# A scheduled attention-and-experts kernel: row maxima scaled on ScalarE, one memset less, and a new order table

## The chip, the cores and the metric

The kernel runs on one core of a Trainium2 chip. A core has five engines that work at the same time, each strictly in the order of its own instruction list: TensorE (PE, products), VectorE (DVE), ScalarE (ACT), GpSimd (POOL) and SyncE (SP, which issues transfers). They wait for each other by semaphores. The metric is the device time of one execution in microseconds (us); lower is better.

## The reference

What is computed, cut to what matters: windowed attention with four sink keys, whose output rows go through a layer of eight experts with two experts for each row.

```python
# q, k, v: (4 batches, 8 heads, 768, 64); n_sink = 4, window = 128
scores = scale * np.matmul(q, k.transpose(0, 1, 3, 2))      # scale = 1 / 8
is_sink = pos[None, :] < n_sink
rel = pos[:, None] - pos[None, :]
scores = np.where(is_sink | ((rel >= 0) & (rel < window)), scores, -1e9)
a = np.exp(scores - scores.max(-1, keepdims=True))
x = matmul(a / (a.sum(-1, keepdims=True) + 1e-9), v)        # rows x: (3072, 512)
logits = x @ w_gate + np.log1p(np.exp(x @ w_noise)) * noise # 8 experts
top2, top2_w = two largest logits of a row, softmax over the two
for e in range(8):                                          # w1: 512 x 1024, w2: 1024 x 512
    out[rows that chose e] += top2_w * (np.maximum(x @ w1[e], 0) @ w2[e])
```

## The kernel before

**Two parts.** Part one is the attention of all four batches, and, for the first three, the routing (which rows go to which expert) and the first gathers of rows. It ends near 172 us. Part two routes the last batch and runs the experts. Both parts share the one clock: part two's operations follow part one's on each engine without a break.

**Steps of the attention.** Heads are taken in pairs, 4 pairs a batch, 16 pairs in all. A step n is 256 queries of one pair; there are 3 steps to a pair, 48 in all. The chain of a step:
- `qk` (L467): TensorE writes scores to one of two PSUM tiles S.
- `cur` (L472, or L474 to L478): VectorE merges the window's two key blocks by masks. The first step of each pair (16 of the 48) has no block before its first one, so there it adds a mask (L474) and overwrites the four sink columns with a large negative value (L475, a memset).
- `mins` (L481): VectorE takes the row maxima, mn. `lowest` (L484): GpSimd multiplies them by -1/8, giving nb (128 partitions by 4).
- `exps` (L489): ScalarE computes four exponentials with nb as bias, and their sums. From there TensorE transposes the probabilities (L525), ScalarE or VectorE copies them (CT, L531, L528), GpSimd or VectorE masks them (CM, L540, L538).
- The four sink columns take a way of their own: copied on ScalarE (L512), their low part formed on GpSimd, and transposed on TensorE (L520) into a PSUM tile X, of which there are three. `pv` (L550, L553) adds the window's products there; dv, the difference of neighbouring blocks of values, is a GpSimd subtraction of 128x640 (recorded at L374, as all of that helper's calls are).
- The result is copied, transposed back and scaled by VectorE into `strip` (L589); that empties X, and the strip goes to DRAM.

**Routing** of a batch is a chain of some fifty small operations (L840 to L988) on VectorE, GpSimd and ScalarE, 6 rows of 8 experts per partition. Its middle: the masks of the chosen experts, m (L867), are counted by TensorE (L875); VectorE forms the place of each row in its expert's list (L917 to L925: 12 columns, among them an and, L922, and a shift, L923, over integers), compares it with a ramp to build wide selection masks (L929, 128x768; L933, 128x336), which GpSimd multiplies with the row numbers (L936) ahead of the product that makes the lists.

**What sets the order.** Operations are handed to a `Plan` with an engine, an estimated duration, a priority and a kind; kind `PORT` marks an operation of which the plan lets only one run at a time over VectorE and GpSimd. In part one the order on each engine is not found by the plan: a table `ORDER` lists the numbers of the operations of each engine, and `in_order` issues them so. While doing that it keeps a clock of its own from the estimated durations, and where that clock shows TensorE idle near the start it puts in filler products (L1821) that compute nothing that is used:

```python
            if ops[i][6] == PORT:
                port = t + d
            start[i] = t
            if e == "PE":
                if idle and t < idle[0]:
                    w = max(free[e], idle[1])
                    fill += [w] * int((t - w) / (idle[2] * (2 if t < self.cold else 1)))
```

Part two is put in order by the plan itself (a list scheduler), with the same kinds of estimates; it takes over the clock that `in_order` ended with. A gather of rows is issued by GpSimd, and `lat` is the time that the plan sets for its landing.

## Time and profile before

| | us |
|---|---|
| median of 3 runs | 723.29 (723.13 to 725.91) |
| the profiled execution | 725.0, span 723.4 |
| TensorE busy | 694.0 (96% of the span) |
| VectorE busy | 536.4 (74%) |
| ScalarE busy | 398.7 (55%) |
| GpSimd busy | 288.4 (40%) |

The profiled execution is one more run, beside the three. Its span is what the engines' records cover; the rest of its time lies around them. Busy shares are means over both parts, whose limits differ, so the stages have to be read one by one. All times in the rows are microseconds from the span's start unless marked ns.

### The profile page before, as it was taken

How to read it: one execution, taken by the hardware profiler on the slowest of the kernel's cores; microseconds unless marked ns; L12 is line 12 of the kernel's file. 1: busy time of each engine (PE TensorE's matmuls, PEld its weight loads, DVE VectorE, ACT ScalarE, POOL GpSimd, SP SyncE). 2: the span in 40 equal slices, each digit the busy share in tenths (PEclk: the TensorE clock that was granted, in tenths of full speed). 3: DMA queues.
4: the chain of work that ended last, by engine and by line, in shares of the span. 5: the costliest groups of instructions: out<-in, count | busy, mean ns of one | idle time of the engine just before them, and what ended most of it. 6: DMA issues, size and time to landing. Idle time of an engine off the chain costs nothing. (4 is left out here: it accounts for less than half of the span.)

```text
span 723.4 us, 13584 instructions
## 1 busy us (share of the span) xinstructions
PE 694.0 (96%) x4752; PEld 586.1 (81%) x4752; DVE 536.4 (74%) x1292; ACT 398.7 (55%) x1067; POOL 288.4 (40%) x431
## 2 busy tenths in 40 slices
PE   7999898988999999999999999999999999999995
PEld 3767666766778889889988998898899889889984
DVE  6789899877734897797797779587967968785720
ACT  5898787855113465555564566365555645654420
POOL 4547577683336352173224215230722530081022
PEclk9999999999999999999999999999999999999998
DMA  7584878847468997477538564864676291254132
GB/s 250 173 252 162 256 207 219 226 104 257 132 188 230 295 291 214 150 137 231 191 85 221 154 193 109 198 176 140 148 196 198 79 251 55 88 112 106 60 44 45
DMA packets 87335, 123.40 MB, mean 171 GB/s; under 512 B 18656, under 2 KB 55392, under 8 KB 87264
## 3 DMA queue, kind: packets, MB, share of 16 engines
q1 hardware_dynamic: 75856, 94.64, 42.1%
q0 software_dynamic: 11408, 27.86, 19.2%
q8 instruction: 38, 0.62, 0.4%
q14 instruction: 33, 0.27, 0.1%
HBM read 81.75 MB, written 40.73 MB: 169 GB/s over the span
## 5 line engine op out<-in xcount | busy, mean ns | idle before, releaser
L1413 POOL DMA_INDIRECT out<-tmp,idx x34 | 80.5, 2366 | 162.2 <-ACT tmp L1398 153.9
L1520 PE MATMUL B<-x,wr 128*128 128x384 f32 (+1 forms) x392 | 134.8, 344 | 1.5 <-DVE x L374 1.5
L1550 PE MATMUL Y<-w2a,hb 128*128 128x512 f32 x504 | 129.2, 395 | 0.0
L1550 PE MATMUL Y<-w2b,hb 128*128 128x512 f32 x504 | 125.4, 392 | 0.7 <-DVE hb L1543 0.7
L1550 PEld LDWEIGHTS Y<-w2b,hb 128*128 128x128 f32 x504 | 94.4, 188 | 21.1 <-DVE hb L1543 1.2
L1550 PEld LDWEIGHTS Y<-w2a,hb 128*128 128x128 f32 x504 | 94.2, 188 | 19.3
L489 ACT ACTIVATE cbuf<-S,nb 128x132 f32<-128x132 f32 x192 | 68.7, 375 | 23.0 <-POOL nb L484 22.7
L1519 PE MATMUL B<-xe,wr 128*128 128x384 f32 (+1 forms) x224 | 76.9, 343 | 1.0 <-ACT tmp L1534 1.0
L1520 PEld LDWEIGHTS B<-x,wr 128*128 128x128 f32 x392 | 73.6, 188 | 5.0 <-DVE x L374 2.3
L1521 PE MATMUL B<-xe,wr 128*128 128x384 f32 (+1 forms) x224 | 76.7, 343 | 0.0
L374 DVE TENSOR_TENSOR wr<-st,wr 128x512 fp32r<-128x512 f32 (+1 forms) x86 | 59.5, 698 | 14.3 <-ACT wr L1231 14.0
L1519 PE MATMUL B<-x,wr 128*128 128x384 f32 (+1 forms) x168 | 57.9, 345 | 1.0 <-DVE tmp L1537 1.0
L1521 PE MATMUL B<-x,wr 128*128 128x384 f32 (+1 forms) x168 | 57.6, 343 | 0.0
L1231 ACT ACTIVATE wr<-st 128x512 fp32r<-128x512 f32 x84 | 52.0, 624 | 8.8 <-DVE st L374 6.5
L1082 POOL COPY spacer<-hb 1x1 f32<-1x1 f32 x38 | 12.5, 328 | 92.5 <-ACT hb L1540 89.6
L1534 ACT ACTIVATE tmp<-B 128x384 f32<-128x384 f32 (+1 forms) x56 | 28.0, 500 | 38.7 <-PE B L1521 34.7
L1398 ACT ACTIVATE tmp<-Y,wc 128x512 f32<-128x512 f32 x31 | 21.3, 688 | 45.7 <-PE Y L1550 33.4
L467 PE MATMUL S<-kq 64*64 64x196 f32 (+2 forms) x768 | 41.7, 328 | 4.2 <-ACT cbuf L489 4.1
L1519 PEld LDWEIGHTS B<-xe,wr 128*128 128x128 f32 x224 | 42.1, 188 | 3.6 <-ACT tmp L1534 1.3
L1413 POOL DMA_INDIRECT out<-turned,idx x17 | 30.1, 1769 | 37.0 <-ACT turned L1398 33.7
L1521 PEld LDWEIGHTS B<-xe,wr 128*128 128x128 f32 x224 | 42.0, 188 | 0.2
L1067 POOL DMA_INDIRECT sg<-x_rows,rt_idi x30 | 30.5, 1018 | 27.7 <-DMA x_sorted<-sg 12.9
(313 smaller groups left out, 1560.7 us busy)
## 6 DMA issues: line engine op xcount, KB each, us to landing
st<-in_w1c SPq DMA_DIRECT2D x32, 512.0 KB, 4.5
st<-in_w2c SPq DMA_DIRECT2D x32, 512.0 KB, 4.4
kq<-in_qk_t SPq DMA_DIRECT2D x15, 780.0 KB, 5.7
...
x_rows<-strip SPq DMA_DIRECT2D x48, 128.0 KB, 3.5
```

The costliest lines, as they stand in the source:

```text
L374: eng.tensor_tensor(out, a, b, op=OP.subtract)
L467: nc.tensor.matmul(whole[x, h, c0:c1], kq(g)[r, KS + 128 * j + 64 * s:KS + 128 * j + 64 * s + 64], kq(g)[r, o + c0:o + c1], start=True, st ...
L489: nc.scalar.activation(C(n)[:, u], S_(n, 0, KW)[:, u // 2, u % 2], AF.Exp, scale=1.0 / math.sqrt(D), bias=get("nb", n)[:, u // 2, u % 2:u ...
L1067: nc.gpsimd.indirect_dma_start(out=stage(), out_offset=None, in_=xbuf, in_offset=bass.IndirectOffsetOnAxis(ap=cst["idw"]()[:, sh.TE * e + ...
L1231: plan.op("ACT", .03 + .255 * m, z, lambda: nc.scalar.activation(h(), src(), AF.Copy), r=[st], w=[(*key, b)] + old, u=[key, ex], lat=P2["s ...
L1398: nc.scalar.activation(get("y", Y[e, t], [128, DM]), get("Y", Y[e, t]), AF.Copy, scale=c["wc"][e % 2][:, t:t + 1])
L1413: d = nc.gpsimd.indirect_dma_start(out=out, out_offset=bass.IndirectOffsetOnAxis(ap=c["idx"][:size(e, t), e, t:t + 1], axis=0), in_=get("y ...
L1519: nc.tensor.matmul(p, wh, h, start=start and not k, stop=False, skip_group_check=True)
L1520: nc.tensor.matmul(p, wh, l, start=False, stop=False, skip_group_check=True)
L1521: nc.tensor.matmul(p, wl, h, start=False, stop=k == 1, skip_group_check=True)
L1534: nc.scalar.activation(u_of(e, k), src(), AF.Copy)
L1550: nc.tensor.matmul(p, h[:, x * (CAP + R) + 128 * t:x * (CAP + R) + 128 * t + 128], w[:, y], start=(f == 0 and x + y == 0), stop=(f == FC - ...
```

## The change

The scaled row maxima are computed by ScalarE instead of GpSimd. The mask added in the first steps becomes 132 columns wide, its last four filled with the large negative value, so that the addition covers the sink columns too and the memset goes; the set-up gains a memset of the wider mask and one for each of the two tiles S, whose sink columns the addition now reads. In the plan, many small operations of the routing (L840 to L1015), the row sums and the copy of the gate weights become `PORT`; estimated durations change a little; landings of the first gathers are set at 5.4 and 4 us for 4.2 and 3. The table `ORDER` of part one is replaced.

```diff
 ORDER = dict(
-    Pool=(0, 17, 13, 26, 55, 22, 34, 28, 68, 32, 95, 70, 64, 76, 103, 59, 74, 105, 111, 135, 99, 143, 109, 170, 183,
+    Pool=(13, 34, 22, 32, 28, 76, 59, 74, 64, 105, 111, 99, 70, 145, 151, 109, 139, 131, 185, 149, 191, 225, 179, 189,
...
-    m0 = consts.tile([128, 128], F32, name="m0")
-    nc.vector.tensor_scalar(m0, jp, 0.0, -BIG, op0=OP.is_gt, op1=OP.mult)
+    m0 = consts.tile([128, KW], F32, name="m0")
+    nc.vector.memset(m0, -BIG)
+    nc.vector.tensor_scalar(m0[:, :128], jp, 0.0, -BIG, op0=OP.is_gt, op1=OP.mult)
...
-            nc.vector.tensor_tensor(S_(n, 0, 128)[:, 0], S_(n, KW, 128)[:, 0], m0[:, None, :].to_broadcast([128, 2, 128]), op=OP.add)
-            nc.vector.memset(S_(n, 128, NS)[:, 0], -BIG)
+            nc.vector.tensor_tensor(S_(n, 0, KW)[:, 0], S_(n, KW, KW)[:, 0], m0[:, None, :].to_broadcast([128, 2, KW]), op=OP.add)
...
     def lowest(n):
-        nc.gpsimd.tensor_scalar(get("nb", n, [128, 2, 2]), get("mn", n), -1.0 / math.sqrt(D), None, op0=OP.mult)
+        nc.scalar.activation(get("nb", n, [128, 2, 2]), get("mn", n), AF.Copy, scale=-1.0 / math.sqrt(D))
...
-            op("DVE", .6 if jj else .8, n + P(n, "cur"), lambda n=n: cur(n), w=[("S", n)])
+            op("DVE", .61 if jj else .98, n + P(n, "cur"), lambda n=n: cur(n), w=[("S", n)])
             op("DVE", .62, n + .4 + P(n, "mins"), lambda n=n: mins(n), r=[("S", n)], w=[("mn", n)])
-            op("Pool", .15, n + .4 + P(n, "sub"), lambda n=n: lowest(n), r=[("mn", n)], w=[("nb", n)])
+            op("ACT", .17, n + .4 + P(n, "sub"), lambda n=n: lowest(n), r=[("mn", n)], w=[("nb", n)])
...
-            op("ACT", 1.55, n + .4 + P(n, "exps"), lambda n=n: exps(n), r=[("S", n), ("nb", n)], w=[("C", n), ("sm", n // 2)])
+            op("ACT", 1.4, n + .4 + P(n, "exps"), lambda n=n: exps(n), r=[("S", n), ("nb", n)], w=[("C", n), ("sm", n // 2)])
...
-                op("Pool", .15, n + .8 + P(n, "sums"), lambda m=m: sums(m), w=[("sm", m)])
+                op("Pool", .25, n + .8 + P(n, "sums"), lambda m=m: sums(m), w=[("sm", m)], kind=PORT)
...
-    dve(lambda: v.tensor_scalar(rt("pp", pair, I32), rt("g"), 127, None, op0=OP.bitwise_and), ["g"], ["pp"], .08)
+    dve(lambda: v.tensor_scalar(rt("pp", pair, I32), rt("g"), 127, None, op0=OP.bitwise_and), ["g"], ["pp"], .09, kind=PORT)
...
-        plan.op("Pool", 1.28, z, go, r=[("idg", int(not first))] + kept * first, w=[row], lat=4.2 if first else 3)
+        plan.op("Pool", 1.28, z, go, r=[("idg", int(not first))] + kept * first, w=[row], lat=5.4 if first else 4)
...
-    plan.op("DVE", .065, z, go, r=[row], w=[("wc", e, t)], u=[("wc", e)])
+    plan.op("DVE", .08, z, go, r=[row], w=[("wc", e, t)], u=[("wc", e)], kind=PORT)
...
                     nc.vector.memset(s[:64, :, a * sh.HALF + sh.NS + 192:a * sh.HALF + sh.NS + 256], 0.0)
+                nc.vector.memset(s[64:, :, sh.HALF + 2 * sh.NS:sh.HALF + 3 * sh.NS], 0.0)
```

What the new table and the moved operation do to the instruction lists is shown at three places, one in the routing of each of the first three batches. After the change, lines from 395 to 473 have numbers higher by one (cur's L472 is L473, its addition L475); from L476 on they are as before. In the names, sm are the row sums, ri their reciprocals, pcbuf the sink columns, z and rt_w the weights of the experts.

GpSimd in the routing of the first batch, up to the dv that stands there, before the change:

```order
L484 TENSOR_SCALAR nb<-mn 128x4
L493 TENSOR_SCALAR sm<-sm 128x8
L374 TENSOR_TENSOR pcbuf<-cbuf,pcbuf 128x16x4
L885 TENSOR_TENSOR z_121<-rt_mx 128x6
L484 TENSOR_SCALAR nb<-mn 128x4
L374 TENSOR_TENSOR dv<-vn 128x640
```

The same stretch after it:

```order
L867 TENSOR_TENSOR m<-oh_122 128x48
L540 AFFINE_SELECT CM<-CT 128x512
L885 TENSOR_TENSOR z_123<-rt_mx 128x6
L540 AFFINE_SELECT CM<-CT 128x512
L493 TENSOR_SCALAR sm<-sm 128x8
L374 TENSOR_TENSOR dv<-vn 128x640
```

The two multiplications nb (L484), each of which waited for row maxima of VectorE, are gone; the one that stood last ahead of dv has only a mask and row sums in its place.

VectorE in the routing of the second batch, before the change (rt_g is a row's place, rt_pp and rt_tq its and and shift, rt_tv a value made of the shift):

```order
L923 TENSOR_SCALAR rt_tq<-rt_g 128x12
L925 SCALAR_TENSOR_TENSOR rt_tv<-rt_tq,rt_vl 128x12
L504 RECIPROCAL ri<-sm 128x4x2
L933 TENSOR_TENSOR rt_tc_1961<-io_94,rt_tv 128x336
L933 TENSOR_TENSOR rt_tc_1964<-io_94,rt_tv 128x336
L474 TENSOR_TENSOR S_83<-S_83,m_167 128x2x128
L475 MEMSET S_83 128x2x4
L476 COPY_PREDICATED S_83<-le,S_83 128x2x128
L478 TENSOR_TENSOR S_83<-S_83,m_169 128x2x4
L922 TENSOR_SCALAR rt_pp<-rt_g 128x12
L481 TENSOR_REDUCE mn<-S_83 128x4
L589 TENSOR_TENSOR strip<-B_78,ri 128x256
```

The same stretch after the change:

```order
L923 TENSOR_SCALAR rt_tq<-rt_g 128x12
L922 TENSOR_SCALAR rt_pp<-rt_g 128x12
L925 SCALAR_TENSOR_TENSOR rt_tv<-rt_tq,rt_vl 128x12
L929 TENSOR_TENSOR rt_op_1955<-io,rt_pp 128x768
L933 TENSOR_TENSOR rt_tc_1967<-io_96,rt_tv 128x336
L504 RECIPROCAL ri<-sm 128x4x2
L475 TENSOR_TENSOR S_83<-S_83,m_169 128x2x132
L476 COPY_PREDICATED S_83<-le,S_83 128x2x128
L478 TENSOR_TENSOR S_83<-S_83,m_172 128x2x4
L589 TENSOR_TENSOR strip<-B_78,ri 128x256
L481 TENSOR_REDUCE mn<-S_83 128x4
L589 TENSOR_TENSOR strip<-B_79,ri 128x256
```

L922 stood nine rows behind L923, right ahead of a row maximum (L481) and two strips (the second is the row behind the last one shown); it now stands right behind L923, with an L929 and one L933 after it, and the two strips no longer follow each other. On GpSimd, the same batch from the copy of a block of expert weights (wr) on, before:

```order
L374 TENSOR_TENSOR wr<-st,wr 128x1024
L484 TENSOR_SCALAR nb<-mn 128x4
L889 TENSOR_TENSOR z_121<-z_121 128x6
L867 TENSOR_TENSOR m<-oh_123 128x48
L540 AFFINE_SELECT CM<-CT 128x512
L885 TENSOR_TENSOR z_124<-rt_mx 128x6
L890 TENSOR_TENSOR rt_wd<-oh_120,z_121 128x96
L892 TENSOR_TENSOR rt_w<-rt_wd 128x48
L493 TENSOR_SCALAR sm<-sm 128x8
L484 TENSOR_SCALAR nb<-mn 128x4
L374 TENSOR_TENSOR pcbuf<-cbuf,pcbuf 128x16x4
```

The rows that follow there:

```order
L887 TENSOR_SCALAR rt_den<-z_124 128x6
L540 AFFINE_SELECT CM<-CT 128x512
L936 TENSOR_TENSOR rt_tc_1961<-rt_tc_1961,tok 128x336
L540 AFFINE_SELECT CM<-CT 128x256
L374 TENSOR_TENSOR dv<-vn 128x640
L493 TENSOR_SCALAR sm<-sm 128x8
```

After the change, from the masks m on:

```order
L867 TENSOR_TENSOR m<-oh_125 128x48
L540 AFFINE_SELECT CM<-CT 128x512
L374 TENSOR_TENSOR wr<-st,wr 128x1024
L374 TENSOR_TENSOR pcbuf<-cbuf,pcbuf 128x16x4
L540 AFFINE_SELECT CM<-CT 128x512
L892 TENSOR_TENSOR rt_w<-rt_wd 128x48
L493 TENSOR_SCALAR sm<-sm 128x8
L936 TENSOR_TENSOR rt_tc_1967<-rt_tc_1967,tok 128x336
L540 AFFINE_SELECT CM<-CT 128x256
L885 TENSOR_TENSOR z_126<-rt_mx 128x6
L374 TENSOR_TENSOR dv<-vn 128x640
L540 AFFINE_SELECT CM<-CT 128x512
```

The wr stood ahead of m and stands behind it now. There is one L936 ahead of dv in both; in the new lists the L936 waits for the L933 that stands behind L922 on VectorE, while in the old ones both L933 stood ahead of L922.

VectorE in the routing of the third batch, before:

```order
L924 TENSOR_SCALAR rt_vl<-r_128 128x12
L922 TENSOR_SCALAR rt_pp<-rt_g 128x12
L923 TENSOR_SCALAR rt_tq<-rt_g 128x12
L925 SCALAR_TENSOR_TENSOR rt_tv<-rt_tq,rt_vl 128x12
L929 TENSOR_TENSOR rt_op_2632<-io,rt_pp 128x768
L933 TENSOR_TENSOR rt_tc_2639<-io_94,rt_tv 128x336
L933 TENSOR_TENSOR rt_tc_2644<-io_94,rt_tv 128x336
L907 TENSOR_TENSOR vm<-slot,B_79 128x4
L589 TENSOR_TENSOR strip<-B_77,ri 128x256
```

After the change:

```order
L924 TENSOR_SCALAR rt_vl<-r_130 128x12
L923 TENSOR_SCALAR rt_tq<-rt_g 128x12
L922 TENSOR_SCALAR rt_pp<-rt_g 128x12
L925 SCALAR_TENSOR_TENSOR rt_tv<-rt_tq,rt_vl 128x12
L929 TENSOR_TENSOR rt_op_2622<-io,rt_pp 128x768
L933 TENSOR_TENSOR rt_tc_2626<-io_96,rt_tv 128x336
L929 TENSOR_TENSOR rt_op_2635<-io,rt_pp 128x768
L933 TENSOR_TENSOR rt_tc_2653<-io_96,rt_tv 128x336
L589 TENSOR_TENSOR strip<-B_77,ri 128x256
```

Ahead of the strip stood one L929 and two L933; now two of each stand there. On ScalarE, each set of four exponentials (L489) now has its nb (L484) ahead of it on the same engine.

## Rows read from the trace of the kernel before

**Rows 1.** the page: busy time, share of the span and instructions of each engine.
```profile
PE 694.0 (96%) x4752; PEld 586.1 (81%) x4752; DVE 536.4 (74%) x1292; ACT 398.7 (55%) x1067; POOL 288.4 (40%) x431
```

**Rows 2.** table by stage (from:to us): length, busy (instructions) per engine, clock, DMA.
```profile
0.00:16.40 16.40, 11.74 (x107) 5.50 (x108) 10.51 (x36) 8.28 (x32) 7.16 (x27) 1.00 0.79 276
16.40:56.00 39.60, 38.80 (x547) 27.66 (x548) 33.06 (x75) 34.82 (x158) 19.14 (x43) 1.00 0.62 197
56.00:96.00 40.00, 36.40 (x521) 27.16 (x521) 37.57 (x102) 30.98 (x143) 25.78 (x52) 1.00 0.64 201
96.00:136.00 40.00, 37.73 (x543) 27.58 (x543) 36.99 (x103) 32.18 (x139) 28.33 (x57) 1.00 0.87 245
136.00:172.00 36.00, 31.84 (x396) 23.94 (x395) 27.25 (x84) 21.75 (x77) 25.43 (x53) 1.00 0.62 177
```

**Rows 3.** what TensorE waits for, whole span: total us, times, longest us.
```profile
PE B L520 <- DVE strip L589: 4.4, 5, 1.3
...
PE B L1145 <- DMA xg<-x_rows,idg: 1.7, 1, 1.7
```

**Rows 4.** timeline: start, duration us, engine, line, [idle before <- releaser].
```profile
74.16 0.26 PE L520 MATMUL B<-idr,pcbuf 128*128 128x128 f32 x1 [1.29 <-DVE strip L589]
...
103.89 2.37 POOL L374 TENSOR_TENSOR wr<-st,wr 128x1024 fp32r<-128x1024 f32 x1
...
112.06 1.54 POOL L374 TENSOR_TENSOR dv<-vn 128x640 f32<-128x640 f32 x1
...
112.18 1.44 DVE L922 TENSOR_SCALAR rt_pp<-rt_g 128x12 int32<-128x12 int32 x1
...
114.62 0.28 PE L520 MATMUL B<-idr,pcbuf 128*128 128x128 f32 x1 [1.33 <-DVE strip L589]
...
151.86 0.28 PE L520 MATMUL B<-idr,pcbuf 128*128 128x128 f32 x1 [1.03 <-DVE strip L589]
```

**Rows 5.** two VectorE lines, all runs: shortest/middle/longest ns, first and last start.
```profile
L922 DVE TENSOR_SCALAR rt_pp<-rt_g x3: 173/1444/1486, 69.7 to 147.7; 128x12 int32<-128x12 int32 x3
...
L923 DVE TENSOR_SCALAR rt_tq<-rt_g x3: 159/172/1509, 72.1 to 149.1; 128x12 int32<-128x12 int32 x3
```

**Rows 6.** groups of instructions, 0 to 171 us: busy us, mean ns | idle before.
```profile
L484 POOL TENSOR_SCALAR nb<-mn 128x4 f32<-128x4 f32 x48 | 17.0, 355 | 44.5 <-DVE mn L481 38.3 <-ACT cbuf L489 1.5 <-DVE strip L589 1.3
...
L475 DVE MEMSET S<- 128x8 f32 x16 | 1.0, 65 | 1.2
...
L886 ACT ACTIVATE z<-z 128x6 f32<-128x6 f32 x3 | 0.6, 213 | 0.9 <-POOL z L885 0.9
```

**Rows 7.** timeline of ScalarE, two dependent small instructions.
```profile
175.47 0.24 ACT L842 ACTIVATE turned<-turned 128x48 f32<-128x48 f32 x1 [2.60 <-DVE turned L840]
175.75 0.24 ACT L843 ACTIVATE turned<-turned 128x48 f32<-128x48 f32 x1
```

**Rows 8.** the table by stage for tile nb alone: ScalarE and GpSimd.
```profile
16.40:56.00 39.60, 22.54 (x120) 4.03 (x14) 1.00 0.62 197
```

**Rows 9.** timeline of the start, several engines.
```profile
6.17 0.43 DVE L474 TENSOR_TENSOR S<-S,m 128x256 f32<-128x256 f32 x1 [1.27 <-PE S L467]
...
7.47 1.47 PE L1821 MATMUL B<-one 128*128 128x512 bf16 x6
...
10.11 0.89 PE L467 MATMUL S<-kq 64*64 64x196 f32 x16 [1.18 <-ACT cbuf L489]
...
12.67 1.19 POOL L484 TENSOR_SCALAR nb<-mn 128x4 f32<-128x4 f32 x1 [2.47 <-DVE mn L481]
...
14.56 0.28 PE L520 MATMUL B<-idr,pcbuf 128*128 128x128 f32 x1 [0.72 <-POOL pcbuf L374]
...
15.47 0.89 PE L467 MATMUL S<-kq 64*64 64x196 f32 x16 [0.63 <-ACT cbuf L489]
```

**Rows 10.** timeline early in the second part, VectorE and GpSimd.
```profile
182.54 2.41 POOL L374 TENSOR_TENSOR w2b<-st,w2b 128x1024 fp32r<-128x1024 f32 x1
182.60 2.38 DVE L920 SCALAR_TENSOR_TENSOR turned<-turned,r 128x12 int32<-128x12 uint32 x1
```

More of the change, by code (lines that the diff above doesn't have):

```diff
@@ L840, in routing @@
     dve(lambda: v.scalar_tensor_tensor(rt("ab", ab_), lg()[:, :, E:], -1.0, lg()[:, :, E:], op0=OP.mult, op1=OP.max),
-        lgk, ["ab"])
+        lgk, ["ab"], kind=PORT)
     act(lambda: nc.scalar.activation(rt("ex", ab_), rt("ab"), AF.Exp, scale=-1.0), ["ab"], ["ex"])
@@ L860, in routing @@
     dve(tops, ["no"], ["mx"], .08 * nt)
-    dve(topi, ["no", "mx"], ["ix"], .14 * nt)
+    dve(topi, ["no", "mx"], ["ix"], .14 * nt, kind=PORT)
     full = [128, 2, nt, E]
@@ L952, in routing @@
         n_ = sh.FA
-        gp_ = lambda fn, r, w: step("Pool", .13, fn, [(x, i) for x in r], [(x, i) for x in w])
+        gp_ = lambda fn, r, w: step("Pool", .17, fn, [(x, i) for x in r], [(x, i) for x in w], kind=PORT)
         gp_(lambda: gp.tensor_scalar(tab("em"), tab("vm"), -1.0, 1.0, op0=OP.mult, op1=OP.add), ["vm"], ["em"])
-        step("Pool", .13, lambda: gp.tensor_tensor(tab("ids"), tab("ids"), tab("vm"), op=OP.mult), [("vm", i)], [("ids", 0)])
+        step("Pool", .17, lambda: gp.tensor_tensor(tab("ids"), tab("ids"), tab("vm"), op=OP.mult), [("vm", i)], [("ids", 0)], kind=PORT)
         gp_(lambda: gp.tensor_tensor(tab("ga"), tab("em"), c["dum"].to_broadcast([128, n_]), op=OP.mult), ["em"], ["ga"])
-        step("Pool", .13, lambda: gp.tensor_tensor(tab("ga"), tab("ga"), tab("ids"), op=OP.add), [("ids", 0)], [("ga", i)])
+        step("Pool", .17, lambda: gp.tensor_tensor(tab("ga"), tab("ga"), tab("ids"), op=OP.add), [("ids", 0)], [("ga", i)], kind=PORT)
         gp_(lambda: gp.tensor_tensor(tab("sa"), tab("em"), tab("spare"), op=OP.mult), ["em"], ["sa"])
-        step("Pool", .13, lambda: gp.tensor_tensor(tab("sa"), tab("sa"), tab("ids"), op=OP.add), [("ids", 0)], [("sa", i)])
-        step("Pool", .1, lambda: gp.tensor_copy(c["m"][:, sh.T:, 0], tab("em")), [("em", i)], [("mx", 0)])
+        step("Pool", .17, lambda: gp.tensor_tensor(tab("sa"), tab("sa"), tab("ids"), op=OP.add), [("ids", 0)], [("sa", i)], kind=PORT)
+        step("Pool", .14, lambda: gp.tensor_copy(c["m"][:, sh.T:, 0], tab("em")), [("em", i)], [("mx", 0)], kind=PORT)
         dve(lambda: v.scalar_tensor_tensor(c["idg"][:, fl], where()[:, fl], 128.0, tab("ga"), op0=OP.add, op1=OP.add),
@@ L1007, in ordered @@
     dve(lambda: v.tensor_reduce(rt("ef", [128, E]), rt("pe"), op=OP.add, axis=AX.X), ["pe"], ["ef"], .13, after=9)
-    dve(lambda: v.tensor_copy(c["eid"], rt("ef")), ["ef"], [("eid", 0)], .07, after=9)
+    dve(lambda: v.tensor_copy(c["eid"], rt("ef")), ["ef"], [("eid", 0)], .07, after=9, kind=PORT)
     dve(lambda: v.tensor_tensor(c["vm"], c["slot"], rt("cp")[:, :, None].to_broadcast([128, E, TE]), op=OP.is_lt),
@@ L1014, in ordered @@
     n = E * TE - sh.FA
-    step("Pool", .28, lambda: gp.tensor_scalar(tab("em"), tab("vm"), -1.0, 1.0, op0=OP.mult, op1=OP.add), [("vm", 1)], [("em", 1)])
+    step("Pool", .28, lambda: gp.tensor_scalar(tab("em"), tab("vm"), -1.0, 1.0, op0=OP.mult, op1=OP.add), [("vm", 1)], [("em", 1)], kind=PORT)
     step("Pool", .28, lambda: gp.tensor_tensor(tab("ga"), tab("em"), c["dum"].to_broadcast([128, n]), op=OP.mult), [("em", 1)], [("ga", 1)], kind=PORT)
     step("Pool", .28, lambda: gp.tensor_tensor(tab("sa"), tab("em"), tab("spare"), op=OP.mult), [("em", 1)], [("sa", 1)], kind=PORT)
-    step("Pool", .28, lambda: gp.tensor_scalar(c["over"], c["most"][:1, :1], 0.0, None, op0=OP.is_gt), [("most", 0)], [("over", 0)])
+    step("Pool", .28, lambda: gp.tensor_scalar(c["over"], c["most"][:1, :1], 0.0, None, op0=OP.is_gt), [("most", 0)], [("over", 0)], kind=PORT)
 def experts_setup(nc, cst, sh, pool):
```

24 lines of the change are left out of this document (12 added, 12 removed), and 96 rows, old and new, of tables (ACT, DVE, PE, Pool).

## The prediction, made before the changed kernel was run

> **What bounds the kernel now.** I read the page's engine shares first [rows 1]: TensorE is busy 694.0 us of 723.4, VectorE 536.4. So at most 29.4 us of the span is TensorE waiting, and a change that leaves the products alone can only take from those. The table by stage [rows 2] says where they lie in the first part, up to 172 us: 4.66 us before 16.4 (16.40 less 11.74), then 0.80, 3.60, 2.27 and 4.16, together 15.5. The granted clock is 1.00 in all of them, so the clock plays no role. The same table shows two other engines close to full: VectorE has 37.57 of 40.00 us from 56 to 96 and 36.99 from 96 to 136, ScalarE 34.82 of 39.60 from 16.4 to 56. In the two middle stages VectorE and TensorE are both near their limit, and whatever stretches a VectorE instruction there is paid by TensorE. The list of what TensorE waits for [rows 3] has one named culprit: L520, the sink transpose, waits 4.4 us in five goes for the strip of VectorE (L589), which must empty the PSUM bank first.
>
> The timeline shows why [rows 4]. At 112.06 GpSimd starts the difference of values, dv (1.54 us). At 112.18 VectorE starts L922, an and over 12 columns, and takes 1.44 us for it, ending (113.62) when dv does (113.60). The same line took 0.173 us in its quickest run and L923, a shift of the same size, 0.159; their slowest are 1.486 and 1.509 [rows 5]. So these small instructions are held for the whole length of a GpSimd instruction that meets them. Behind them stand the row maximum and the strip, and TensorE waits 1.33 us until 114.62. It happens in each of the three routed batches: 1.29 us before 74.16, 1.33 before 114.62, 1.03 before 151.86, together 3.65.
>
> **What the change does, part by part.**
>
> *The scaled maxima (L484) go from GpSimd to ScalarE.* GpSimd loses 48 instructions and 17.0 us; they took 355 ns on the mean [rows 6]. ScalarE gains 48 of 4 columns. No such instruction runs there now; the nearest is L886, 6 columns, 213 ns [rows 6]. The exponentials follow it on the same engine and need its result: L842 and L843, two dependent small ones, stand 0.28 us apart (175.47, 175.75) [rows 7]. So a new one takes 0.21 to 0.28 us of ScalarE, 10.2 to 13.4 us in all. In the fullest stage, where 14 of them stand [rows 8], ScalarE goes from 34.82 to 37.8 or 38.7 of 39.60. It still fits; an engine at 96% that works strictly in order will make TensorE wait now and then, and I put 0.5 us on the path there (bounds 0, since it fits, and 3.9, the 14 at 0.28 with no cover). What is hidden is hidden by TensorE's own work of 38.80 us in that stage.
>
> The Trainium skill's page "ScalarE: Activation LUTs" (Rules for kernel authors) speaks against this edit: a multiplication belongs on VectorE, and an ACTIVATE with a bias taken by pointer is to be budgeted at about 0.3 us plus 0.83 ns for each element. By that figure, an estimate from the page, the fullest stage would hold 34.82 + 14 x 0.3 = 39.0 of 39.60. No row of this kernel shows such a multiplication on ScalarE.
>
> The gain lies where GpSimd was held. At 12.67 [rows 9] its nb took 1.19 us beside a VectorE instruction, and TensorE then waited 0.72 us at 14.56 and 0.63 at 15.47. With 0.21 to 0.28 on ScalarE that nb is some 0.9 us shorter. Bounds: 0, and 1.35, both waits; I take 0.8, since the delay taken away is nearer to the upper one. In other places nb's usual way (GpSimd) and the new one cost about the same.
>
> *One memset less in `cur`.* L475 was 16 instructions, 1.0 us busy, with 1.2 us of idle time in front of them [rows 6]. The addition before it now covers 264 columns for 256: by its 0.43 us [rows 9], 0.013 us more, 0.2 in all. VectorE gains 0.8 to 2.0 us over four batches; TensorE sees of that only what falls in the full stages. Bounds 0 and 2.0, I take 0.4, near the lower end, since the waits of those stages come from elsewhere. Three memsets more in the set-up cost nothing: VectorE sat idle 1.27 us before its first addition at 6.17. Without that cover they would cost some 0.3.
>
> *Three more filler products at the start.* The plan's fillers run at 0.245 us each (six in 1.47 us from 7.47), 0.74 us for three. They hide in the 1.18 us in which TensorE waits before 10.11; uncovered they would cost 0.74. I take nothing.
>
> *Port kinds and new durations.* In part one each engine's order is the table's, so these costs do not set it; they count the fillers and hand their clock to part two, which is scheduled with them. What counts in part one is the table.
>
> *The new table at the three collisions.* In batch 0 the old row had nb, which waited for the maxima, directly ahead of dv on GpSimd, so dv came as late as those maxima did, beside the wide L929 and then L923. Now nothing there waits for them; dv can be over when L922 and L923 come. I take 0.9 of the 1.29. In batch 1 the old row had dv free to run beside L922. In the new one dv stands behind L936, which multiplies what L933 makes, and L933 stands behind L922 and L923 on VectorE: those two cannot meet. But a copy of weights (wr), which ran 2.37 us from 103.89 [rows 4], before the mask product m (L867) of this batch, now stands behind m and one L540, and the chain from m to L922 goes on meanwhile; if it is quick, L919 to L922 meet wr. I take 0.8 of the 1.33. In batch 2 dv stands later too, but VectorE now has four wide instructions (two L929, two L933) ahead of the strip where three were, so the strip may be as late as before: 0.2 of the 1.03. Together 1.9; bounds 0 and 3.65.
>
> *The rest of the table.* The first gathers stand a little ahead of where they were against the last mask (L540); the wait for their landing is 1.7 us [rows 3]. Bounds 0 and 1.7; I take 0.2, because four gathers still go out one after the other. The sum of the last pair, which moves behind the gathers, is needed only by the last strips and by the gate sums. All other TensorE waits from 16.4 to 172 come to 10.83 - 3.65 - 1.73 = 5.45 us; a new order drops some and makes others. I take nothing, bounds 2.5 either way, about half.
>
> *Part two.* Its order moves as well. At 182.60 VectorE's L920 took 2.38 us, held by the weight split on GpSimd (2.41 us from 182.54) [rows 10], and now that split starts sooner against the routing. Such shifts move waits of 1 us or so; I take nothing, bounds 1.5 either way. The products there are the same, and TensorE is full, so what part one gains or loses comes out at the end.
>
> **Sum.** -0.8 - 0.4 - 1.9 - 0.2 + 0.5 = -2.8 us. The profiled run took 725.0 us (span 723.4), which would be 722.2; it lies 1.7 above the median of the three, 723.29, and the same step from there gives 720.5.
>
> **Rivals.**
> - *The collisions move instead of going.* dv has to run somewhere, VectorE is 94% full in the stage with two of the three, and four wide instructions now stand together in batch 2. For it: held instructions are seen in every batch, and wr is longer than dv. Against it: the pairs of batches 0 and 1 are parted in the rows. Then -0.8 - 0.4 - 0.2 + 0.5 leaves -0.9: 722.4.
> - *ScalarE becomes the bound, and it gets slower.* nb waits for VectorE's maxima at the head of ScalarE's queue, and the copies behind it wait too. The place is 16.4 to 56: spare there is 4.78 us for 14, so from 0.34 us each it costs. At 0.6 us each it takes 3.6 and eats the gains. At 0.75 it takes 5.7 there and, with 14 taken in the next two stages too, 1.5 from 56 to 96 (30.98 + 10.5 against 40) and 2.7 from 96 to 136 (32.18 + 10.5), 9.9 in all, less the 3.3 gained elsewhere: 729.9. For it: ScalarE's fill and the strict order. Against: 0.21 to 0.28 in the nearest rows, and the exponentials waited for nb at the same place before. The page's budget for an ACTIVATE above would bring the stage to its edge, not over it.
> - *All of it goes.* The three collisions (3.65), both waits at the start (1.35), 0.4 of the memsets and half of the other waits (2.7), less nothing for ScalarE: -8.1, 715.2. For it: these waits have the same few causes. Against: half of those others have no link to the port.
> - *The costs in the plan do nothing.* True for part one by themselves, as said; then only the table and the two edits count, which the forecast has already.
>
> **How the numbers follow.** Forecast, -1.5 to -6: 0.50. Collisions move: 0.25. All goes: 0.13. ScalarE binds: 0.12. The likeliest gives 720.5, with its own range 717.3 to 721.8. The range for 8 in 10 goes from 715.4, near the case in which all goes, to 725.0, past the moved collisions by the 2.5 that the rest of the table may cost; it leaves out most of the ScalarE case and the far end of the other. A change of 0.5% is 3.6 us, about what a measurement here tells from none: faster is below 719.7, slower above 726.9. Of the forecast's -1.5 to -6 half lies below 719.7 (0.25), with 0.13 of the case in which all goes: faster 0.38. Slower 0.11, nearly all of the ScalarE case. The rest, 0.51, is same.
>
> **What would show it.** In the new profile: L484 on ScalarE near 0.21 us, ScalarE at 37 to 39 us in the stage up to 56 with TensorE's waits there below 1.5; L922 and L923 near 0.17 us in batches 0 and 1; L520's waits for the strip down from 4.4 to about 2; TensorE's part one ending 2 to 3 us sooner, and part two as long as before. I am wrong if L919 to L923 still last as long as dv or wr, if TensorE's waits for the exponentials grow by several us, or if part two's waits change by more than 2 us.

## The result, and the profile after

The changed kernel takes 716.61 us (median of 4 runs, 715.63 to 718.88), the kernel before 724.01 (4 runs beside it): ratio 0.9899, 95% interval 0.9867 to 0.9931, 7.4 us faster. Seven further runs on another chip gave 717.72 against 725.02, ratio 0.9907 (0.9874 to 0.9939). The profiled run took 718.88 us, span 717.2.

The page's engine shares, as in [rows 1]:

```profile
PE 692.4 (97%) x4755; PEld 586.5 (82%) x4755; DVE 530.8 (74%) x1279; ACT 403.6 (56%) x1115; POOL 281.4 (39%) x383
```
The table by stage, as in [rows 2]:

```profile
0.00:16.40 16.40, 13.30 (x130) 6.97 (x132) 12.14 (x40) 9.86 (x43) 6.04 (x23) 1.00 0.80 276
16.40:56.00 39.60, 39.21 (x572) 28.95 (x570) 33.91 (x74) 36.81 (x181) 17.53 (x31) 1.00 0.71 220
56.00:96.00 40.00, 39.28 (x565) 29.36 (x558) 38.21 (x104) 35.77 (x163) 21.26 (x43) 1.00 0.72 227
96.00:136.00 40.00, 37.71 (x540) 27.91 (x540) 35.70 (x105) 32.28 (x146) 24.97 (x49) 1.00 0.69 188
136.00:172.00 36.00, 32.76 (x353) 24.60 (x350) 27.65 (x101) 21.67 (x74) 19.53 (x40) 1.00 0.76 228
```
TensorE's waiting in the five stages (length less busy) is 3.10, 0.39, 0.72, 2.29 and 3.24, together 9.7 for 15.5 before. VectorE is as full as it was in the second and third (33.91, 38.21), and ScalarE is fuller: 36.81 of 39.60 and 35.77 of 40.00. Up to 56 us TensorE has done 702 products, before 654; three of the 48 more are fillers. So its lead is larger than its shorter waits; whether short gaps between products, counted as busy, make the difference isn't shown.

What TensorE waits for, as in [rows 3]:

```profile
PE B L1519 <- ACT tmp L1534: 3.5, 3, 2.0
PE B L761 <- DVE strip L589: 1.5, 2, 0.8
PE B L875 <- DVE m L867: 1.4, 1, 1.4
...
PE B L1145 <- DMA xg<-x_rows,idg: 1.2, 2, 0.7
PE S L468 <- ACT cbuf L489: 1.0, 3, 0.4
PE S L468 <- DVE mn L481: 1.0, 1, 1.0
```
L520 no longer waits for the strip. Two waits for a strip stand at the gate product instead (L761, 0.72 us before 126.57 and 0.83 before 159.96), so 4.4 us of such waits have become 1.5. The first and the third row lie in the second part; there the first was 1.0 us in one go before, and the third is new.

The small instructions of [rows 5], with the L920 beside them:

```profile
L920 DVE SCALAR_TENSOR_TENSOR rt_g<-rt_ix,r x3: 174/176/1082, 65.8 to 140.6; 128x12 int32<-128x12 uint32 x3
...
L922 DVE TENSOR_SCALAR rt_pp<-rt_g x3: 156/164/165, 67.5 to 140.9; 128x12 int32<-128x12 int32 x3
...
L923 DVE TENSOR_SCALAR rt_tq<-rt_g x3: 159/172/173, 67.6 to 140.8; 128x12 int32<-128x12 int32 x3
```
L922 and L923 are at 0.16 to 0.17 us in all three batches. The hold is not gone everywhere: one L920, at 65.8, took 1.08 us beside a dv. TensorE waited for no strip there.

The groups of [rows 6] up to 171 us; columns as there:

```profile
L489 ACT ACTIVATE cbuf<-S,nb 128x132 f32<-128x132 f32 x192 | 68.4, 372 | 0.9
...
L484 ACT ACTIVATE nb<-mn 128x4 f32<-128x4 f32 x48 | 10.0, 208 | 11.3 <-DVE mn L481 10.7
...
L475 DVE TENSOR_TENSOR S<-S,m 128x264 f32<-128x264 f32 x16 | 6.9, 434 | 1.6 <-PE S L468 0.8 <-ACT CT L531 0.6 <-ACT pcbuf L512 0.3
```
The new instruction on ScalarE takes 208 ns, 10.0 us in all. Two rows that I had not read in the kernel before are that of the exponentials, same view, and that of all its nb, in the columns of [rows 5]:

```profile
L489 ACT ACTIVATE cbuf<-S,nb 128x132 f32<-128x132 f32 x192 | 68.7, 375 | 23.0 <-POOL nb L484 22.7
```
```profile
L484 POOL TENSOR_SCALAR nb<-mn x48: 212/226/1188, 8.3 to 155.8; 128x4 f32<-128x4 f32 x48
```
Before, ScalarE stood idle for 23.0 us in front of the exponentials (6.3 of them before the first), nearly all for nb from GpSimd. Now it is 0.9 there and 11.3 in front of the nb themselves (5.3 of them before the first), where it waits for the maxima: 12.2 for 23.0. Of these 10.8 us less the nb's own work fills 10.0, so the idle time shows the place and not the size of the gain. The second row shows more of it. Most nb took 0.23 us on GpSimd, and the mean of 355 ns comes from eight that took 0.47 to 1.19, each beside a wide VectorE instruction: the one of 12.67 to 13.86 ran beside VectorE's L426 (12.51 to 13.78).

The last transpose of part one (L580) marks where TensorE leaves the attention. Both kernels, before first (shortest/middle/longest ns, first and last start in us):

```profile
L580 PE MATMUL B<-idf,turned x96: 272/273/329, 21.1 to 166.6; 128*128 128x128 f32 x96
```
```profile
L580 PE MATMUL B<-idf,turned x96: 272/273/330, 18.3 to 158.5; 128*128 128x128 f32 x96
```
Part one ends 8.1 us sooner (166.6 and 158.5), the whole 6.2 in these two executions (spans 723.4 and 717.2). From that transpose to the end it takes 558.7 us where it took 556.8: in these two the second part gives 1.9 us back. One execution says little here. In all traces of the runs below together with these two, the five with the old lists of the second part take 551.4 to 556.8 us from that transpose on (middle 555.1), the seven with the new ones 553.5 to 560.8 (middle 559.6).

### The profile page after: what moved, and what is told of

It is laid out like the page before. It is cut to its first block, busy times and chain, and to the rows that moved or that the text cites. A ratio compares the mean times of both kernels' runs of the same rounds, so it can differ in the third digit from the quotient of the medians.

```text
span 717.2 us, 13573 instructions
## 1 busy us (share of the span) xinstructions
PE 692.4 (97%) x4755; PEld 586.5 (82%) x4755; DVE 530.8 (74%) x1279; ACT 403.6 (56%) x1115; POOL 281.4 (39%) x383
## 4 chain that ended last, share of the span: by engine, by line
PE 74%; DMA 9%; DVE 5%; ACT 3%; issue 3%; POOL 3%; SPq 0%; POOLq 0%; DVEq 0%; ACTq 0%
PE Y L1550 31%; PE B L1519 9%; PE B L1520 9%; PE B L1521 9%; PE S L468 3%; DMA xg<-x_sorted 3%; ACT cbuf L489 2%; DMA x_rows<-strip 2%; PE B L550 2%; DMA sg<-x_rows,idg 2%; PE Y L1553 2%; PE B L525 1%; DMA vn<-in_v 1%; PE B L553 1%; DMA xg<-x_rows,idg 1%
## 5 line engine op out<-in xcount | busy, mean ns | idle before, releaser
L1413 POOL DMA_INDIRECT out<-tmp,idx x34 | 87.1, 2562 | 153.3 <-ACT tmp L1398 149.1
L1519 PE MATMUL B<-xe,wr 128*128 128x384 f32 (+1 forms) x224 | 77.2, 345 | 3.5 <-ACT tmp L1534 2.2
L489 ACT ACTIVATE cbuf<-S,nb 128x132 f32<-128x132 f32 x192 | 68.4, 372 | 0.9
L1519 PE MATMUL B<-x,wr 128*128 128x384 f32 (+1 forms) x168 | 57.9, 345 | 1.3 <-ACT tmp L1534 1.3
L1519 PEld LDWEIGHTS B<-xe,wr 128*128 128x128 f32 x224 | 42.0, 188 | 7.3 <-ACT tmp L1534 3.1
L1413 POOL DMA_INDIRECT out<-turned,idx x17 | 31.9, 1876 | 36.9 <-ACT turned L1398 33.8
L1534 ACT ACTIVATE tmp<-B 128x384 f32<-128x384 f32 (+1 forms) x56 | 27.7, 499 | 32.3 <-PE B L1521 27.8
L1540 ACT ACTIVATE hb<-B 128x384 fp32r<-128x384 f32 (+1 forms) x56 | 28.0, 502 | 27.9 <-DVE B L1537 13.3
```

The costliest lines, as they stand in the source:

```text
L489: nc.scalar.activation(C(n)[:, u], S_(n, 0, KW)[:, u // 2, u % 2], AF.Exp, scale=1.0 / math.sqrt(D), bias=get("nb", n)[:, u // 2, u % 2:u ...
L1413: d = nc.gpsimd.indirect_dma_start(out=out, out_offset=bass.IndirectOffsetOnAxis(ap=c["idx"][:size(e, t), e, t:t + 1], axis=0), in_=get("y ...
L1519: nc.tensor.matmul(p, wh, h, start=start and not k, stop=False, skip_group_check=True)
L1534: nc.scalar.activation(u_of(e, k), src(), AF.Copy)
L1540: nc.scalar.activation(hx(e, f, 0, j), src(), AF.Relu)
```

## The experiments

Each ran beside the kernel before on one chip. "Mean clock" is the mean granted TensorE clock of an execution. The kernel before ran 66 times here: 724.4, 725.0 and 724.7 us on the three chips.

**The maxima on ScalarE, in the old table.** 48 numbers of the table move from GpSimd's row to ScalarE's.

```diff
-        nc.gpsimd.tensor_scalar(get("nb", n, [128, 2, 2]), get("mn", n), -1.0 / math.sqrt(D), None, op0=OP.mult)
+        nc.scalar.activation(get("nb", n, [128, 2, 2]), get("mn", n), AF.Copy, scale=-1.0 / math.sqrt(D))
...
-    Pool=(0, 17, 13, 26, 55, 22, 34, 28, 68, 32, 95, 70, 64, 76,
+    Pool=(0, 13, 22, 34, 28, 32, 70, 64, 76,
...
-    ACT=(19, 12, 27, 21, 33, 56,
+    ACT=(17, 19, 12, 26, 27, 21, 33, 55, 56,
```

> The kernel before, with the scaled maxima on ScalarE, each right ahead of its exponentials; the rest of the old table and all else as before (two more filler products). Theory A (the maxima's shorter way to the exponentials is what pays): 3 to 5 us faster than before, 719 to 721, with the lead already there by the sixteenth step. Theory B (the new table pays, by parting held VectorE instructions from dv): 0 to 1 us faster, 723 to 724. Theory C (ScalarE becomes the bound by itself, and only the new table makes room for it): 1 to 3 us slower.

Measured: 720.47 us, ratio 0.9947 (0.9927 to 0.9967), 3.9 us faster. The exponentials' group up to 171 us, the last transpose, and the first stage:

```profile
L489 ACT ACTIVATE cbuf<-S,nb 128x132 f32<-128x132 f32 x192 | 68.5, 369 | 1.9
```
```profile
L580 PE MATMUL B<-idf,turned x96: 272/273/330, 20.9 to 163.8; 128*128 128x128 f32 x96
```
```profile
0.00:16.40 16.40, 13.21 (x110) 6.74 (x110) 10.70 (x37) 9.07 (x36) 6.11 (x23) 0.90 0.75 276
```
ScalarE's 23 us of waiting fall to 1.9 there (10.7 in front of the nb come to it), and part one ends 2.8 us sooner although TensorE's clock was at 0.90 on the mean in the first stage, which costs up to 0.10 x 16.4 = 1.6 us. Theory A holds for this edit, and C falls. The collisions have no part in it: in batch 0 the hold moved to L920 (1.42 us), and TensorE still waits 1.27, 1.24 and 0.98 us at the three places. The lead was not all there by the sixteenth step, though: that maximum started 1.2 us sooner than before, the last but two 3.5 us sooner, so it grows over part one. Summed over the 48 steps, the way from the end of a maximum to its first exponential is 29.6 us for 34.2. Of these 4.6 us, 4.2 lie at the eight steps whose nb GpSimd took 0.47 to 1.19 us for, 0.3 at the other forty: what pays is mostly that nb is no longer held. No run tests that by itself.

**All but the new table.** The changed kernel with the old table, nb ahead of its exponentials.

```diff
-    Pool=(13, 34, 22, 32, 28, 76, 59, 74,
+    Pool=(0, 13, 22, 34, 28, 32, 70, 64,
...
```

> The changed kernel with the old table, the maxima put right ahead of their exponentials in ScalarE's list: all of the change but the new order of part one (the second part is ordered by the new costs). Theory A: 718 to 720. Theory B: 721 to 723. Theory C: slower than before.

Measured: 720.76 us, 0.9959 (0.9937 to 0.9981), like the run before it, between the ranges of A and B. Part one ends at 161.5:

```profile
L580 PE MATMUL B<-idf,turned x96: 272/273/330, 20.4 to 161.5; 128*128 128x128 f32 x96
```
So in these traces the table is worth 3.0 us in part one on top of the other edits (158.5), A and B each hold for a part, and since a reordered second part comes with it (555.8 us here, in an order that neither kernel has), the time doesn't show what the wide addition does by itself.

**Two VectorE instructions parted from dv.** In the table of the kernel before:

```diff
-        366, 509, 367, 368, 510, 375, 372, 369, 370,
+        366, 509, 367, 368, 369, 510, 375, 372, 370,
...
-        655, 657, 659, 722, 664, 661, 838, 656, 839,
+        655, 657, 656, 659, 722, 664, 661, 838, 839,
```

> The kernel before, with two VectorE instructions moved in its table: L923 of the first routed batch right behind L922, and L922 of the second batch right behind L923; nothing else. Theory B: both are at 0.17 us instead of 1.5, TensorE's two waits for the strip (1.29 and 1.33 us) shrink, 1.7 to 2.6 us faster than before. The rival (the lock moves to the next VectorE instruction that meets dv): 0 to 0.5 us faster.

Measured: 723.38 us, 0.9982 (0.9964 to 1.0000): 1.3 us by the ratio, with an interval that reaches no change. Both lines, then the timeline of batch 0:

```profile
L922 DVE TENSOR_SCALAR rt_pp<-rt_g x3: 172/180/1490, 72.1 to 149.4; 128x12 int32<-128x12 int32 x3
...
L923 DVE TENSOR_SCALAR rt_tq<-rt_g x3: 160/164/175, 72.2 to 150.8; 128x12 int32<-128x12 int32 x3
```
```profile
73.86 2.21 POOL L374 TENSOR_TENSOR dv<-vn 128x640 f32<-128x640 f32 x1
...
74.60 1.50 DVE L924 TENSOR_SCALAR rt_vl<-r 128x12 f32<-128x12 f32 x1
...
76.58 0.25 PE L520 MATMUL B<-idr,pcbuf 128*128 128x128 f32 x1 [1.29 <-DVE strip L589]
```
The moved instructions are quick (the one left at 1.49 is batch 2's). In batch 1 TensorE's wait for the strip is gone (two of 0.29 and 0.58 for exponentials follow). In batch 0 the hold moved to the next small instruction behind the wide ones: L924, 1.50 us, ends with dv, and TensorE waits the same 1.29. So the rival was right for one place, theory B for the other. The Trainium skill's page "SBUF — State Buffer" (SBUF: two separate sides) calls the port pair that VectorE and GpSimd share an exclusive lock for a whole instruction, where the VectorE instruction has two inputs in SBUF or runs in a two-port mode. The trace agrees on the whole instruction, with L924 ending within 0.03 us of dv; L924 has one input, and no run here shows its mode. This run also showed something else:

```profile
0.00:16.40 16.40, 11.78 (x107) 5.42 (x107) 10.56 (x36) 8.90 (x35) 7.44 (x27) 0.95 0.76 276
16.40:56.00 39.60, 38.84 (x517) 28.27 (x517) 30.85 (x67) 31.82 (x144) 17.00 (x41) 0.93 0.60 194
```
The clock was at 0.95 and 0.93 in the first two stages, at 1.00 in the profile before. This execution lost 0.05 x 16.4 + 0.07 x 39.6 = 3.6 us by that at most.

**The maxima back on GpSimd, in the new table.** Their 48 numbers go back to GpSimd's row, at the places that the plan's clock gives.

```diff
...
-        nc.scalar.activation(get("nb", n, [128, 2, 2]), get("mn", n), AF.Copy, scale=-1.0 / math.sqrt(D))
+        nc.gpsimd.tensor_scalar(get("nb", n, [128, 2, 2]), get("mn", n), -1.0 / math.sqrt(D), None, op0=OP.mult)
```

> The changed kernel with the scaled maxima back on GpSimd, at the places that the plan's clock gives; TensorE's and VectorE's order as in the changed kernel. Theory A: 3 to 5 us slower than the changed kernel, 720 to 722. Theory B: 0 to 1 us slower, 716.5 to 718. Theory C: faster than the changed kernel, 714 to 716.

Measured: 724.01 us, 0.9993 (0.9978 to 1.0009), the kernel before's time and slower than each theory had it. The waiting for nb is back:

```profile
L489 ACT ACTIVATE cbuf<-S,nb 128x132 f32<-128x132 f32 x192 | 68.7, 374 | 22.5 <-POOL nb L484 21.9
```
```profile
L580 PE MATMUL B<-idf,turned x96: 272/273/330, 22.2 to 165.0; 128*128 128x128 f32 x96
```
```profile
0.00:16.40 16.40, 13.00 (x108) 7.11 (x108) 10.78 (x37) 8.08 (x30) 7.01 (x25) 0.93 0.79 276
16.40:56.00 39.60, 38.58 (x532) 28.20 (x524) 30.78 (x64) 33.30 (x154) 17.10 (x42) 0.94 0.64 197
```
The clock fell here too, at 0.93 and 0.94, up to 3.5 us, and once more in the second part (334.8 to 338.2 us, up to 1.7). That mixes with the effect, hence the runs with fillers below. Also, nb starts 0.42 us after its maximum on the mean here, 0.20 in the kernel before: the new order was not made for nb on GpSimd.

**The changed kernel again.** No edit.

> The changed kernel itself once more, on the chip of the runs beside it, for more executions of it. Theory D (part of the gain is the granted clock: with TensorE idle for 3.4 us in all between 9 and 16 us, most executions of the kernel before fall to the lower level once near the start, and the changed kernel, idle for 1.8 us there, doesn't): mean clock of 0.996 or more in nearly all executions, 716 to 718. Without theory D its clocks spread like those of the kernel before (21 of 30 below 0.996).

Measured: 717.72 us, 0.9907. Mean clocks 0.998, 0.995, 0.998, 0.995, 0.998, 0.994, 0.994: not nearly all at 0.996, as theory D had it. Of all 11 executions of the changed kernel 4 are below, of the 66 of the kernel before 48, and those 48 take 725.0 us in the median, the other 18 take 723.2. So the clock seems to be part of the gain, but a small one: an estimate from these groups is (48/66 - 4/11) x 1.8 = 0.7 us. It takes all of the difference between the groups for the clock's doing, which no run shows.

**More fillers in the kernel before.**

```diff
-WARM = 13.0
+WARM = 16.0
```

> The kernel before with filler products put in up to 16 us on the plan's clock in place of 13 (8 more, all between 10 and 16 us); every other list as before. Theory D: the mean clock is 0.996 or more in most executions, 1 to 2 us faster than before, 722 to 723.5. Rival: the clock stays as spread as before, and the fillers cost up to 8 x 0.245 = 2 us, 724 to 726.

Measured: 721.26 us, 0.9957 (0.9939 to 0.9975), 3.1 us by the ratio, mean clock 0.997 (10 of 12 at 0.996 or more). In the trace part one ends as before:

```profile
L580 PE MATMUL B<-idf,turned x96: 272/273/330, 20.8 to 166.4; 128*128 128x128 f32 x96
```
So the fillers keep the clock up and are worth 3.1 us, more than either expectation had. The clock, estimated as above, explains (48/66 - 2/12) x 1.8 = 1.0 of these; where the other 2.1 come from is open. In the two traces the clock is at 1.00 near the start in both, and the whole difference lies behind that transpose, in the same lists: 551.4 us for 556.8, with 4.0 us of TensorE's waits for 8.5.

**Fewer fillers in the changed kernel.**

```diff
-WARM = 13.0
+WARM = 10.0
```

> The changed kernel without the 11 filler products behind its second set of scores (8 are left at the very start). TensorE's order is otherwise the same, and the fillers filled a wait, so without theory D the time stays, 716 to 717.5. Theory D: the clock falls near the start in most executions, mean clock below 0.996, 2 to 4 us slower than the changed kernel, 718.5 to 721.

Measured: 718.71 us, 0.9904 (0.9877 to 0.9931). That is the lower edge of what theory D had, but only 1.0 us above the changed kernel beside it, which the intervals don't tell from none. The clock fell as theory D had it (5 of 6 below 0.996), to 0.79 in the first stage:

```profile
0.00:16.40 16.40, 12.04 (x105) 6.75 (x105) 11.38 (x38) 9.43 (x39) 6.30 (x23) 0.79 0.80 276
```
The low clock lay from 8.2 to 15.0 us. From 8 to 15 TensorE was busy 5.67 of 7.00 us, ScalarE 6.59, and part one ended at 157.2, sooner than the changed kernel's 158.5. So here half the clock had no cost that shows, where ScalarE was the fuller engine. The execution with the lowest mean clock of the six (0.989) was the fastest, 714.74.

**Each nb twice.** The same instruction once more, 48 in all.

```diff
         nc.scalar.activation(get("nb", n, [128, 2, 2]), get("mn", n), AF.Copy, scale=-1.0 / math.sqrt(D))
+        nc.scalar.activation(get("nb", n, [128, 2, 2]), get("mn", n), AF.Copy, scale=-1.0 / math.sqrt(D))
```

> The changed kernel with every scaled maximum computed twice on ScalarE (48 instructions of 0.21 us more, 10 us of ScalarE in part one). Rival of the prediction (ScalarE at the edge): 3 to 9 us slower than the changed kernel, 720 to 726, TensorE's waits for the exponentials between 16 and 96 us growing by several us. With room left on ScalarE: 0 to 2 us slower, 716.5 to 719.

Measured: 718.77 us, 0.9931 (0.9901 to 0.9960), 1.1 us above the changed kernel beside it. Three stages:

```profile
16.40:56.00 39.60, 38.22 (x521) 28.00 (x522) 30.69 (x64) 35.64 (x176) 13.10 (x26) 0.94 0.62 196
56.00:96.00 40.00, 38.95 (x550) 28.98 (x550) 37.98 (x103) 36.91 (x168) 22.63 (x44) 1.00 0.69 212
96.00:136.00 40.00, 38.69 (x554) 28.50 (x552) 36.16 (x103) 35.53 (x171) 23.92 (x45) 1.00 0.77 224
```
With 10 us more work ScalarE is 92% full in the second of them, and TensorE waits only 1.38, 1.05 and 1.31 us. In the first, the rival's place, the clock was at 0.94, so that row tests it less well. Part one ends at 163.3 in this trace, 4.8 us later than in the changed kernel's; a low clock up to 56 us explains at most 0.07 x 16.4 + 0.06 x 39.6 = 3.5 of these. The second part, in the changed kernel's lists, took 553.5 us, the least of the seven. So the doubled work is not free in part one, but it costs far less than the 3 to 9 us of a ScalarE that binds.

**Fillers with the changed kernel, with the moved maxima alone, and with the new table alone.** Three kernels; the last two are those of the runs above with the maxima moved.

```diff
-WARM = 13.0
+WARM = 16.0
```

> The changed kernel with filler products up to 16 us on the plan's clock (8 more), as in the run that did so with the kernel before. If the clock near the start still costs the changed kernel something in some executions (4 of 11 were below 0.996): mean clock 0.997, 0.5 to 1.5 us faster than the changed kernel, 715.5 to 717, faster than both kernels. Rival (its waits there are too short to hold fillers): fillers delay work, 0 to 2 us slower, 717 to 719.

> The kernel before with the scaled maxima on ScalarE and fillers up to 16 us: against the kernel before with the fillers alone (721.3) it shows what the moved maxima do in the old table without a fall of the clock. Chain theory (a shorter way from maximum to exponentials, worth 3 us at the end of part one in the trace): 718 to 719. If most of the 3.8 us were the clock: 720.5 to 721.5.

> The changed kernel with the maxima on GpSimd and fillers up to 16 us. Its first run stood at 724.0 with a low clock in 11 of 12 executions. If the new table is of use without the moved maxima: 718 to 720, below the kernel before with the same fillers (721.3). If the new table needs ScalarE's maxima: 721 to 723.

Measured: 719.64 us (0.9934, 0.9919 to 0.9948), 718.18 (0.9917, 0.9894 to 0.9940) and 725.10 (1.0005, 0.9987 to 1.0024). The last transposes, in this order:

```profile
L580 PE MATMUL B<-idf,turned x96: 272/273/330, 17.9 to 156.6; 128*128 128x128 f32 x96
```
```profile
L580 PE MATMUL B<-idf,turned x96: 272/273/330, 20.8 to 163.3; 128*128 128x128 f32 x96
```
```profile
L580 PE MATMUL B<-idf,turned x96: 272/273/331, 19.4 to 163.1; 128*128 128x128 f32 x96
```
The moved maxima are worth 3.1 us once more, with the clock up: 718.18 against 721.26 (2.9 by the ratios, since the chips differ), and 163.3 against 166.4 at the end of part one. The new table with the wide addition ends part one 3.3 us sooner too (163.1 against 166.4), so it doesn't need ScalarE's maxima there, against the theory; its time is no better all the same, since what follows takes 560 us (723.3 - 163.1), with a fall of the clock from 332.6 to 336.0. The changed kernel with more fillers has the shortest part one of all (156.6) and is slower than without: 716.8 - 156.6 = 560.2 us follow. Both expectations of a gain failed, and in the traces both gains are lost in the second part.

**The old costs in the second part.** Wherever the second part uses them, the costs and kinds are those of before, but for the 5.4 us set for the first gather's landing; part one is the changed kernel's, instruction for instruction.

```diff
-        ["ix", "r2"], ["g"], .09, kind=PORT)
+        ["ix", "r2"], ["g"], .08 if last else .09, kind=0 if last else PORT)
...
-        plan.op("Pool", 1.28, z, go, r=[("idg", int(not first))] + kept * first, w=[row], lat=5.4 if first else 4)
+        plan.op("Pool", 1.28, z, go, r=[("idg", int(not first))] + kept * first, w=[row], lat=5.4 if first else 3)
...
-    plan.op("DVE", .08, z, go, r=[row], w=[("wc", e, t)], u=[("wc", e)], kind=PORT)
+    plan.op("DVE", .065, z, go, r=[row], w=[("wc", e, t)], u=[("wc", e)])
```

> The changed kernel with the old costs and kinds wherever the second part uses them (routing of the last batch, gathers, gate weights); part one's lists and fillers are the same. If the reordered second part gives back some of part one's lead (in the traces it lasts 556.0 and 558.8 us from the last transpose of part one in the changed kernel, 551.4 to 556.8 with the old order): 1 to 2.5 us faster than the changed kernel, 715 to 716.5. Rival (it was chance): within 0.7 us of it, 716.5 to 718.

Measured: 713.22 us (713.14 to 714.46), 0.9846 (0.9832 to 0.9860): 11.5 us faster than before, the fastest of all. Its last transpose, and what TensorE waits for from 172 us on:

```profile
L580 PE MATMUL B<-idf,turned x96: 272/273/330, 17.9 to 157.7; 128*128 128x128 f32 x96
```
```profile
PE B L1520 <- DVE x L374: 1.7, 2, 1.1
PE B L1145 <- DMA sg<-x_rows,idg: 0.8, 1, 0.8
PE Y L1550 <- DVE hb L1543: 0.7, 1, 0.7
PE B L1519 <- DVE tmp L1537: 0.6, 1, 0.6
```
The rest takes 711.6 - 157.7 = 553.9 us for 558.7. The changed kernel's largest wait, 3.5 us for ScalarE's copy L1534, is gone. Where two of its three goes came from, in the changed kernel's timeline:

```profile
320.41 1.06 ACT L1190 ACTIVATE w2a<-st 128x1024 fp32r<-128x1024 f32 x1 [2.42 <-DMA st<-in_w2c]
321.38 0.50 ACT L1534 ACTIVATE tmp<-B 128x416 f32<-128x416 f32 x1
...
321.93 0.46 PE L1519 MATMUL B<-x,wr 128*128 128x416 f32 x1 [1.31 <-ACT tmp L1534]
...
323.06 0.71 DVE L1273 STREAM_TRANSPOSE turned<-xg 128x512 f32<-128x512 f32 x1 [3.28 <-DMA xg<-x_sorted]
...
326.47 0.45 PE L1519 MATMUL B<-xe,wr 128*128 128x416 f32 x1 [2.00 <-ACT tmp L1534]
```
ScalarE stands for 2.42 us at the copy of a weight (L1190) whose transfer hasn't landed; the copy that TensorE needs (L1534) is behind it in the queue, and TensorE waits 1.31 us. Then VectorE stands for 3.28 us at a transpose (L1273) of rows that haven't landed; ScalarE's next copies come behind what VectorE does after that, and TensorE waits 2.00 us. With the old costs the first two stand the other way round:

```profile
321.48 0.52 ACT L1534 ACTIVATE tmp<-B 128x416 f32<-128x416 f32 x1 [0.67 <-PE B L1521]
...
322.65 1.06 ACT L1190 ACTIVATE w2a<-st 128x1024 fp32r<-128x1024 f32 x1 [0.22 <-DMA st<-in_w2c]
```
The expectation's gain is met and exceeded: 3.4 to 4.5 us (713.2 against 716.6 and 717.7 on other chips; the intervals of the ratios don't meet). The second part's lists are then those of the kernel before, but for a few instructions at the border of the parts. Which of the costs turned them isn't settled: they were put back together. The new lists don't always cost that: with each nb twice they ran without a wait at L1519.

## Why the prediction was right in direction and small in size

720.5 was forecast and 716.6 measured, inside the range of 715.4 to 725.0 but below the likeliest case's own 717.3 to 721.8; the forecast's 2.8 us were 7.4. Part one was to end 2 to 3 us sooner and ended 8.1 sooner, the sum of the case in which all goes, by other terms. That the time lies inside the range is in part luck: the second part took 3.4 to 4.5 us back, where the forecast put nothing, and without that it lies below the range (713.2).

- **The maxima.** Right that they move well to ScalarE, wrong by a factor of four in size. The step that failed: "In other places nb's usual way (GpSimd) and the new one cost about the same", with 0.8 us for the start alone. In the old table it is 3.1 us with the clock up. The two instructions were compared by 355 and 213 ns, and the mean of the first hid eight that were held; the start was one of the eight. For the other forty the sentence is right: the way from a maximum to its first exponential is 25.1 us for them in all before, and 24.8 with the maxima moved in the old table.
- **ScalarE's load.** Its busy time and TensorE's waits were forecast well (36.81 us where 37.8 to 38.7 was said, waits below 1.5). The 0.5 us on the path are not there: TensorE's waiting in that stage fell from 0.80 to 0.39. That ScalarE becomes the bound is refuted by the moved maxima alone (3.9 us faster) and by the doubled instruction, whose cost stayed near 1 us.
- **The memset.** Not measured by itself. Between the kernels with the old table and nb on ScalarE, with it (163.8 less 1.6 for the clock, and 163.3) and without (161.5), part one ends 0.7 to 1.8 us sooner. But TensorE's wait of 1.24 us for the strip in batch 1 is gone there too, so whether 0.4 was right stays open. The addition is at 434 ns, as forecast.
- **The collisions.** L520's 4.4 us for the strip are gone, and 1.5 us at L761 are new: 2.9 less where 1.9 was forecast. The mechanism is shown by the run that parts two of them, and so is the rival: what is held can change. wr (101.07 to 103.43 in the changed kernel) met none of the small instructions, L919 to L922, since they came after it (from 104.25).
- **The rest of the table.** 0 was put; the table as a whole, collisions included, is 3.0 us in part one, and 3.3 with the wide addition, within what the terms and the bound of 2.5 allow. The wait for the gathered rows fell from 1.7 to 1.2, 0.2 was put.
- **The second part.** "I take nothing, bounds 1.5 either way" failed: the new costs put weights ahead of copies and take 3.4 to 4.5 us (713.2 against 716.6 and 717.7; up to (4/7) x 1.8 = 1.0 of the larger figure may be the clock, by the estimate above). Without that the time lies below even the case in which all goes (715.2).
- **The clock.** That "the clock plays no role" was read from one execution. Over 66 executions those with the lower clock take 1.8 us more in the median, and the estimate is about 0.7 us of the gain.

In the two profiled executions part one gives 8.1 and the second part takes 1.9, of a span 6.2 shorter; in the second trace of the changed kernel, against the same trace of before, part one gives 8.4 (it ends at 158.2) and the second part 0.9 more (555.9). So part one's gain is firm, and the second part's share in one execution is not.
